# One fused SSM and gated-GLU kernel: PSUM read two banks at a time, paired products, and a new order

## The chip, the cores and the metric

One core of a Trainium2 chip runs the whole program. The time is device microseconds, the median of several runs. The engines are TensorE (PE), VectorE (DVE), ScalarE (ACT), GpSimd (POOL) and SyncE (SP), which issues most of the DMAs. Each has its own queue and works through it in order. [...]

## The reference

A layernorm of x (2048 tokens, 512 channels) feeds two branches that are added to x: a diagonal state-space layer, computed as a convolution over the whole length, and a gated linear unit.

```python
xn = layernorm(x)                                   # 2048 x 512
# branch A: K[d, l] = Re sum_n C[d,n] * exp(dt*A)[d,n]**l * (dt*B)[d,n],  128 modes, l = 0..2047
y  = irfft(rfft(pad(xn)) * rfft(pad(K)))[:L] + xn * Dskip
# branch B: 512 -> 1792 -> 512
h  = sigmoid(xn @ w_gate) * (xn @ w_up)
out = x + y + h @ w_down
```

Inputs and outputs are bfloat16; sums on PE are float32.

## The kernel before, in words

**Branch B** works on four groups of 512 tokens. For each group and each of 14 blocks of 128 hidden columns PE makes a gate product (L1031, four matmuls of 128x512) and an up product (L1046), each in one PSUM bank. ACT takes the sigmoid of the gate bank into `hT_sb` (L1040). DVE multiplies by the up product (L1061), straight from its bank or, for the blocks in the list `UEV`, from a copy `us_sb` that ACT has made of it (L1057). Then come the down products (L1090), 14 matmuls for each of four blocks of 128 tokens.

**Branch A** does the long convolution by transforms written as matmuls. A ladder of complex squares (ACT L656, DVE L665 and L667, twelve levels) gives powers of the decay; POOL's DMAs cast them into tables. From these DVE builds two factor tables G and H in four chunks of 128 channels (L722 to L728 products, L775 to L781 squares, seeds copied by `copy`, L291 and L293). PE multiplies them (L806), ACT brings the result to SBUF, PE selects and transposes it (L827). On the other side PE makes the first transform of the layernormed tokens (L684), ACT evacuates it, and SP writes it to DRAM (`z_scr`) and reads it back in another layout. For 8 unit pairs in two channel halves PE then makes a second step (L874) and the kernel's transform from streamed constants E (L890), ACT or DVE evacuates both, DVE multiplies them (L895, L899), sums some parts (L906, L907, L909) and PE makes the third step (L923, L935). How much is summed on DVE is the table `SUMS`: at level 0 PE gets 64 matmuls a pair, at level 1 32, at level 2 16. ACT's copies of that go to DRAM (`v_scr`) and come back, and PE makes the last transform (L999); DVE adds it to branch B (L1014, L1110), and the sum is stored.

**PSUM** has eight banks of 512 float32 columns. Each is a tile of its own, and every evacuation reads one bank: `halves` makes two copies of 128x512 out of two banks.

**The order** is written out by hand. `_Plan.add` lists 981 operations with the bank or buffer slots that each takes and gives back; the table `ORDER` says in which order they are handed to the engines, and `run` gives out slots first come, first served as it goes along that order. `ON_DVE` and `ON_ACT` name operations that change the engine, `WARM` the warm-up matmuls (L520) on a zero tile. So all of an engine's queue, and which bank a product gets, follows from these tables.

```python
def halves(dst, srcs, deps, prio, hold):
    cps = []
    for n, sl in enumerate(srcs):
        cps.append(pl.copy(nc, 0.48, lambda n=n: dst(n), lambda sl=sl: bank(sl), deps + cps, prio, acq=[] if n else [hold], rel=[sl]))
    return cps
```

## Time and profile before

| | |
|---|---|
| runs | 214.62, 214.68, 215.55 us; median 214.68 |
| profiled execution | span 212.7 us (first to last instruction); its own time is not on the page |
| busy | PE 204.5 us, DVE 196.0, ACT 176.8, POOL 40.5 |
| DMA | 42.35 MB, 199 GB/s in the mean |
| costliest | evacuations by ACT L293 81.5 us; gate products 53.8, up 53.1, down 50.4 |

"Busy" is time in which an engine had an instruction running; for PE the ends are modelled, so that a busy stretch can still hold gaps. DVE's and ACT's instructions are shown with a tail that overlaps the next one; the distance from one start to the next start is what an instruction takes from its queue. The releaser of a wait is what ended it last. The chain of waits is followed back from the last instruction, so it tells what could not have been earlier, and not all that was busy.

### The profile page before, as it was taken

Reading aid. Unit: us, or ns where it says so; the run is one execution under the profiler, and the core shown is the slowest. Engines: PE = TensorE matmul, PEld = TensorE weight load, DVE = VectorE, ACT = ScalarE, POOL = GpSimd, SP = SyncE. Lnnn points to the kernel's source line nnn. Section 1 sums busy time; section 2 is a strip of 40 time slices with the busy share of each in tenths; the row PEclk is TensorE's granted clock in tenths of the full one; section 3 lists DMA queues with packets and bytes.
Section 4 is the critical chain, followed back from the end, with each engine's and each line's share of the span. In section 5 each row is a group of like instructions: output and inputs, shape, how many; then the busy total and the mean of one; then the engine's idle time right before and its main releaser. Section 6 shows DMA issues by size and latency. Waiting matters only on the chain.

```text
span 212.7 us, 5732 instructions
## 1 busy us (share of the span) xinstructions
PE 204.5 (96%) x2226; PEld 103.6 (49%) x2251; DVE 196.0 (92%) x420; ACT 176.8 (83%) x364; POOL 40.5 (19%) x66
## 2 busy tenths in 40 slices
PE   7999999999999999999999999999999999999993
PEld 2574444444444354545456555644565446444442
DVE  3999999999999999999999999999999989984781
ACT  3999999999999999969999999898589999644000
POOL 4206033149877000002000002000040000000110
PEclk9999999999999999999999999999999999999999
DMA  6999937992995927987626446602899996778842
GB/s 205 385 411 349 292 85 166 195 205 33 195 201 195 208 98 223 145 250 265 151 70 216 125 152 166 160 6 60 256 306 222 329 303 188 206 216 230 248 158 91
DMA packets 44044, 42.35 MB, mean 199 GB/s; under 512 B 8809, under 2 KB 37746, under 8 KB 44018
## 3 DMA queue, kind: packets, MB, share of 16 engines
q1 hardware_dynamic: 39074, 36.95, 56.7%
q0 software_dynamic: 4512, 4.73, 14.3%
q8 instruction: 17, 0.28, 0.6%
q10 hardware_dynamic: 432, 0.33, 0.5%
q14 instruction: 9, 0.07, 0.1%
HBM read 25.21 MB, written 12.07 MB: 175 GB/s over the span
## 4 chain that ended last, share of the span: by engine, by line
PE 58%; ACT 33%; DMA 3%; issue 2%; DVE 1%; SPq 0%; POOL 0%; ACTq 0%; POOLq 0%
PE bank L1090 17%; PE bank L1046 11%; ACT big L293 10%; PE bank L1031 8%; PE bank L890 7%; ACT hT_sb L1040 7%; ACT big L656 5%; DMA xnT<-x_scr 3%; PE bank L806 3%; PE bank L520 3%; ACT glu_sb L536 2%; PE bank L923 2%; PE bank L999 2%; PE bank L935 2%; ACT glu_sb L535 2%
## 5 line engine op out<-in xcount | busy, mean ns | idle before, releaser
L293 ACT ACTIVATE big<-bank 128x512 bf16<-128x512 f32 (+2 forms) x147 | 81.5, 655 | 6.1 <-PE bank L806 2.5
L1031 PE MATMUL bank<-xnT,wg_sb 128*128 128x512 bf16 (+1 forms) x234 | 53.8, 361 | 1.2 <-ACT xnT L293 0.4
L1046 PE MATMUL bank<-xnT,wu_sb 128*128 128x512 bf16 x216 | 53.1, 379 | 0.8 <-ACT us_sb L1057 0.2
L1090 PE MATMUL bank<-wd_sb,hT_sb 128*128 128x512 bf16 (+1 forms) x231 | 50.4, 366 | 0.6 <-DVE hT_sb L1061 0.2
L1040 ACT ACTIVATE hT_sb<-bank 128x512 bf16<-128x512 f32 x56 | 34.7, 655 | 1.0 <-PE bank L1031 1.0
L1031 PEld LDWEIGHTS <-wg_sb 128*128 128x128 bf16 x244 | 22.8, 98 | 25.4 <-issue 4.5
L1090 PEld LDWEIGHTS <-hT_sb 128*128 128x128 bf16 x238 | 22.6, 98 | 25.5 <-issue 2.3
L1046 PEld LDWEIGHTS <-wu_sb 128*128 128x128 bf16 x224 | 21.4, 98 | 26.3 <-issue 2.1
L722 DVE TENSOR_TENSOR big<-big 128x1024 bf16<-128x1024 bf16 (+4 forms) x40 | 26.7, 667 | 0.2
L723 DVE TENSOR_TENSOR big<-big 128x1024 bf16<-128x1024 bf16 (+4 forms) x40 | 26.5, 663 | 0.0
L1057 ACT ACTIVATE us_sb<-bank 128x512 bf16<-128x512 f32 x31 | 21.8, 703 | 3.1 <-DVE rz L970 2.4
L895 DVE TENSOR_TENSOR big<-big 128x2048 bf16<-128x2048 bf16 x16 | 19.4, 1221 | 1.3 <-ACT big L293 0.6
L890 PE MATMUL bank<-big 128*128 128x256 bf16 x160 | 19.7, 273 | 0.6 <-ACT big L293 0.4
L890 PEld LDWEIGHTS <-big 128*128 128x128 bf16 x160 | 15.3, 98 | 5.7 <-DMA big<-c_E 1.1
L661 POOL DMA_DIRECT2D big<-big x24 | 13.0, 550 | 23.1 <-DVE big L667 14.4
L293 ACT ACTIVATE big<-big 128x256 bf16<-128x256 bf16 x34 | 16.8, 520 | 0.2 <-PE bank L806 0.2
L775 ACT ACTIVATE sq_sb<-big 128x256 bf16<-128x256 bf16 (+2 forms) x20 | 14.6, 744 | 2.7 <-DVE big L728 2.0
L727 DVE TENSOR_TENSOR big<-big 128x512 bf16<-128x512 bf16 (+4 forms) x40 | 16.5, 413 | 0.0
L728 DVE TENSOR_TENSOR big<-big 128x512 bf16<-128x512 bf16 (+4 forms) x40 | 16.5, 412 | 0.0
L1061 DVE TENSOR_TENSOR hT_sb<-hT_sb,bank 128x512 bf16<-128x512 bf16 x25 | 16.4, 677 | 0.0
L1061 DVE TENSOR_TENSOR hT_sb<-hT_sb,us_sb 128x512 bf16<-128x512 bf16 x31 | 12.9, 419 | 1.3 <-ACT us_sb L1057 1.3
L495 POOL TENSOR_TENSOR ln_ri<-ln_ve,half 128x4 f32<-128x4 f32 (+2 forms) x6 | 10.8, 1795 | 10.7 <-ACT ln_ve L537 8.4
(99 smaller groups left out, 222.2 us busy)
## 6 DMA issues: line engine op xcount, KB each, us to landing
big<-c_E SPq DMA_DIRECT2D x16, 320.0 KB, 5.0
z_scr<-big SPq DMA_DIRECT2D x16, 256.0 KB, 3.1
big<-z_scr SPq DMA_DIRECT2D x16, 256.0 KB, 3.8
v_scr<-big SPq DMA_DIRECT2D x16, 256.0 KB, 3.6
big<-big POOLq DMA_DIRECT2D x24, 128.0 KB, 3.5
big<-in_A_u_dram SPq DMA_DIRECT2D x4, 512.0 KB, 7.7
big<-v_scr SPq DMA_DIRECT2D x4, 512.0 KB, 4.0
wu_sb<-in_B_w_up_dram SPq DMA_DIRECT2D x2, 896.0 KB, 10.1
```

The lines of the kernel that those rows point to most:

```text
L293: nc.scalar.activation(out=get(out), in_=get(in_), func=ACT.Identity)
L722: V.tensor_tensor(out=wide(outp), in0=wide(lo), in1=mre, op=ALU.mult)
L723: V.tensor_tensor(out=wide(tb()), in0=wide(lo), in1=mim, op=ALU.mult)
L727: V.tensor_tensor(out=outp[:, :, 0], in0=outp[:, :, 0], in1=tb()[:, :, 1], op=opr)
L890: T.matmul(bank(sk[kt == NKT - 1])[:, DW * c:DW * c + DW], es()[:, c, kt, :], kT[p][:, kt, :], start=kt in (0, NKT - 1), stop=kt >= NKT - 2)
L895: V.tensor_tensor(out=pp()[:, :, 0:4, :], in0=xx()[:, :, 0, :].unsqueeze(2).to_broadcast([128, 2, 4, DW]), in1=kb().unsqueeze(1).to_broadc ...
L1031: T.matmul(bank(sl)[:, c0:c1], w_at(w, CUT_G, kt, k), xnT[:, grp, kt, c0:c1], start=(kt == 0), stop=(kt == KT - 1))
L1040: S.activation(out=hT_sb[:, hs.idx, k % 2, :], in_=bank(sl), func=ACT.Sigmoid)
L1046: T.matmul(bank(sl), w_at(wu_sb, CUT_U, kt, k), xnT[:, grp, kt, :], start=(kt == 0), stop=(kt == KT - 1))
L1057: S.activation(out=us_sb[:, us.idx, :], in_=bank(sl), func=ACT.Identity)
L1061: V.tensor_tensor(out=h(), in0=h(), in1=us_sb[:, us.idx, :] if on else bank(sl), op=ALU.mult)
L1090: T.matmul(bank(po)[:, 0:c[1] - c[0]], hT_sb[:, hts[k // 2].idx, k % 2, jj * 128:(jj + 1) * 128], wd_sb[:, k, c[0]:c[1]], start=first and ...
```

## The change

- The eight banks become one tile `banks`, and `joint(a, b)` is a view of 1024 columns where two slots are neighbours. Operations with `pairs=True` get neighbouring slots; single ones are taken by preference from slots without a free neighbour (`LONE`).
- `halves`, the two copies after L806 and the two after L827 become one instruction each that reads both banks, on ACT or DVE.
- Up and gate products are handled by pairs of blocks: `UPS` says for each of the 28 pairs whether ACT copies both, one or none of the up products, and whether DVE multiplies 512 or 1024 columns at once; `GATES` names three pairs whose sigmoid reads both banks. The matmuls are the same.
- The last transform is made for each channel half by itself (24 matmuls of 512 columns become 48 of 256), and DVE adds in place, so that the output buffer there falls away.
- Layernorm tiles 2 and 3 are normalized one by one; `ON_ACT` moves the statistics of six tiles to ACT, not seven, and tile 1 instead of 2 among the first four. Seeds are copied three groups at a time, `LAG0`, `EXP` and the list of `squares` are rearranged for that. The loads of E wait for the lower powers only (`w_low`). `SUMS` of the second half goes from (1, 2, 1, 1) to (1, 1, 2, 2).
- `ORDER` is another one, of 896 operations.

```diff
-SUMS = ((0, 0, 0, 1), (1, 2, 1, 1))
+SUMS = ((0, 0, 0, 1), (1, 1, 2, 2))
...
-UEV = (5, 11, 15, 16, 18, 21, 22, 24, 25, 27, 28, 29, 30, 31, 32, 33, 34, 35, 36, 37, 38, 39, 41, 42, 43, 44, 45, 47, 49, 53, 54,)
-ON_DVE = (95, 96, 97, 109, 118, 181, 194, 375, 485, 488, 494, 507, 551, 587, 598, 600,)
-ON_ACT = (2, 8, 9, 10, 11, 13, 15,)
+UPS = (2, 0, 0, 0, 0, 2, 0, 2, 5, 2, 6, 5, 0, 2, 4, 2, 4, 3, 2, 6, 3, 2, 0, 6, 3, 4, 4, 5)
+GATES = (0, 10, 15)
+ON_DVE = (99, 100, 101, 102, 112, 170, 180, 181, 182, 262, 434, 508, 797)
+ON_ACT = (1, 6, 8, 9, 11, 14)
 ORDER = [
-    1, 21, 23, 0, 24, 25, 29, 30, 2, 35, 26, 19, 27, 3, 5, 6, 31, 34, 43, 44, 32, 28, 36, 10, 14, 20, 22, 37, 40, 38, 33,
+    0, 2, 3, 6, 10, 14, 24, 25, 7, 4, 26, 36, 27, 21, 1, 5, 30, 31, 32, 42, 23, 33, 19, 28, 11, 43, 9, 48, 44, 34, 49,
...
+    def _pair(self, free, a, b):
+
+        best = min(((max(i, free.index(x + 1)), x) for i, x in enumerate(free) if x + 1 in free), default=None)
+        a.idx, b.idx = (best[1], best[1] + 1) if best else free[:2]
...
-            for s in op.acq:
-                s.idx = self.free[s.pool].pop(0)
+            for n, s in enumerate(op.acq):
+                free = self.free[s.pool]
+                if s.pool == "b" and op.pairs:
+                    if n % 2 == 0:
+                        self._pair(free, s, op.acq[n + 1])
+                elif s.pool == "b":
+                    at = min(range(len(free)), key=lambda i: i + LONE * (free[i] - 1 in free or free[i] + 1 in free))
+                    s.idx = free.pop(at)
...
-    banks = [psum.tile([128, 512], F32, name="bank%d" % i) for i in range(NBK)]
+    banks = psum.tile([128, 512 * NBK], F32, name="banks")
...
+    def joint(a, b):
+        return banks[:, 512 * a.idx:512 * a.idx + 1024] if b.idx == a.idx + 1 else None
...
-        cps = []
-        for n, sl in enumerate(srcs):
-            cps.append(pl.copy(nc, 0.48, lambda n=n: dst(n), lambda sl=sl: bank(sl), deps + cps, prio, acq=[] if n else [hold], rel=[sl]))
-        return cps
+        def parts(v, each):
+            return v if joint(*srcs) is not None else [each(n) for n in range(2)]
+        return [pl.copy(nc, 0.96, lambda: parts(dst(), lambda n: dst()[:, 512 * n:512 * n + 512]),
+                        lambda: parts(joint(*srcs), lambda n: bank(srcs[n])), deps, prio, acq=[hold], rel=srcs)]
...
     layernorm(1, 2, 1.05)
-    layernorm(2, 4, 1.1)
+    layernorm(2, 3, 1.1)
+    layernorm(3, 4, 1.15)
...
-            le = dma("SP", es, cten["E"].ap()[u], deps=w_use[0], prio=QP - 0.5, acq=[esl], pkt=2560, hv=0.9)(320 * KB)
+            le = dma("SP", es, cten["E"].ap()[u], deps=w_low[0], prio=QP - 0.5, acq=[esl], pkt=2560, hv=0.9)(320 * KB)
...
+        for p in range(NP):
+            sl = _Slot("b")
+            part = res[:, :, DW * p:DW * p + DW]
+
+            def fy(sl=sl, p=p):
+                for r in range(2):
+                    s2_mm(t, r, bank(sl)[:, DW * r:DW * r + DW], True, (DW * p, DW * p + DW))
+
+            def fe(sl=sl, part=part):
+                V.tensor_tensor(out=part, in0=bank(sl).rearrange("p (r d) -> p r d", r=2), in1=part, op=ALU.add)
...
+            cps = {0: (), 1: (), 2: (0, 1), 3: (0, 1), 4: (0,), 5: (1,), 6: (0, 1)}[mode]
...
+                    for x in [None] if len(do) == 2 and (cps or joint(*ub) is not None) else do:
+                        src = u2v() if x is None and cps else joint(*ub) if x is None else half2(u2v(), x) if x in cps else bank(ub[x])
+                        o_ = h2() if x is None else half2(h2(), x)
+                        V.tensor_tensor(out=o_, in0=o_, in1=src, op=ALU.mult)
```

What the tables do is seen in the queues. First ACT at the start, from the statistics of its first layernorm tile to the table load ahead of the sines (`xnT` are the copies of transposed tiles, L609/L638 and L615/L644 two steps of the decay's phase and size). Before:

```order
L535 ACTIVATE glu_sb,mv<-big 128x512
L536 ACTIVATE glu_sb,mv<-big,mv 128x512
L537 ACTIVATE ln_ve<-mv,eps 128x1
L602 ACTIVATE big<-big 128x512
L293 ACTIVATE xnT<-bank_66 128x4x128
L293 ACTIVATE xnT<-bank_67 128x4x128
L609 ACTIVATE big<-big,magic 128x512
L293 ACTIVATE xnT<-bank_70 128x4x128
L293 ACTIVATE xnT<-bank_63 128x4x128
L615 ACTIVATE big<-big 128x512
L618 ACT_TABLE_LOAD
```

Now:

```order
L557 ACTIVATE glu_sb,mv<-big 128x512
L558 ACTIVATE glu_sb,mv<-big,mv 128x512
L559 ACTIVATE ln_ve<-mv,eps 128x1
L631 ACTIVATE big<-big 128x512
L298 ACTIVATE xnT<-banks 128x4x128 x2
L638 ACTIVATE big<-big,magic 128x512
L644 ACTIVATE big<-big 128x512
L298 ACTIVATE xnT<-banks 128x4x128 x2
L647 ACT_TABLE_LOAD
```

The exponential stands ahead of the copies of tiles 2 and 3 now, and the first three rows are those of tile 1, not 2. On PE the eight transposes of these two tiles are split: ahead of each four stand eight gate halves of 256 columns, and the four warm-up matmuls between them are gone.

They stand further down on PE, among the last up products of group 0 (L1108, L1046 before), ahead of the last-but-one first transforms of that stretch (L711, L684 before). Before:

```order
L1046 MATMUL bank_68<-xnT,wu_sb 128x512
L684 LDWEIGHTS big
L684 MATMUL bank_69<-big 64x512
...
L684 MATMUL bank_67<-big 64x512
L1090 LDWEIGHTS hT_sb
L1090 MATMUL bank_65<-wd_sb,hT_sb 128x512
```

Now, as one piece:

```order
L1108 MATMUL banks<-xnT,wu_sb 128x512
L542 LDWEIGHTS glu_sb
L542 MATMUL banks<-glu_sb 128x512
...
L1108 LDWEIGHTS wu_sb
...
L542 MATMUL banks<-glu_sb 128x512
L711 LDWEIGHTS big
L711 MATMUL banks<-big 64x512
...
L1083 MATMUL banks<-xnT,wg_sb 128x512
L1161 LDWEIGHTS hT_sb
```

Two warm-up matmuls stand on each side of the last up product, and a gate product of group 1 (L1083) comes ahead of the first down products (L1161). Last, ACT in the second channel half, where the second step and the kernel's transform are evacuated. Before:

```order
L293 ACTIVATE big<-bank_68 128x512
L293 ACTIVATE big<-bank_63 128x512
L293 ACTIVATE big<-bank_66 128x512
L293 ACTIVATE big<-bank_65 128x512
L293 ACTIVATE big<-bank_67 128x512
L293 ACTIVATE big<-bank_64 128x512
L1040 ACTIVATE hT_sb<-bank_68 128x512
```

Now:

```order
L298 ACTIVATE big<-banks 128x1024
L1099 ACTIVATE hT_sb<-banks 128x512 x2
L298 ACTIVATE big<-banks 128x1024 x5
L1099 ACTIVATE hT_sb<-banks 128x512
L298 ACTIVATE big<-banks 128x1024 x3
```

Two rows of 512 have become one of 1024, and both banks come back after it.

## The prediction

> **What bounds the kernel now.** I read the page's busy table first, then its 40 slices.

> ```profile
> span 212.7 us, 5732 instructions
> PE 204.5 (96%) x2226; PEld 103.6 (49%) x2251; DVE 196.0 (92%) x420; ACT 176.8 (83%) x364; POOL 40.5 (19%) x66
> DVE  3999999999999999999999999999999989984781
> ACT  3999999999999999969999999898589999644000
> ```

> The span is 212.7 us and the three runs have a median of 214.68, so 1.98 us lies outside the span; the page prints no other time of its execution. A measurement of this kernel tells a change from none from about 0.5%, 1.07 us. PE is busy for 204.5 us. VectorE (DVE) and ScalarE (ACT) are nearly full as well up to slice 33 (176 us), and have room only after that. Next, four stretches of the span (the pairs are each engine's busy time and instructions, then comes the granted clock), and the longest waits of PE alone:

> ```profile
> 0.00:20.00 20.00, 18.22 (x101) 10.01 (x103) 15.80 (x38) 15.98 (x27) 6.29 (x20) 1.00 0.92 340
> 20.00:60.00 40.00, 39.20 (x194) 17.26 (x197) 39.83 (x95) 39.61 (x83) 19.27 (x25) 1.00 0.80 172
> 20.00:200.00 180.00, 176.95 (x2062) 88.25 (x2084) 173.66 (x372) 160.78 (x338) 32.62 (x44) 1.00 0.72 187
> 200.00:212.70 12.70, 9.36 (x66) 5.31 (x65) 6.58 (x12) 0.00 (x0) 1.59 (x2) 0.98 0.40 148
> ...
> PE bank L520 <- POOL glu_sb L506: 1.4, 1, 1.4
> PE bank L890 <- ACT big L293: 0.4, 1, 0.4
> PE bank L1031 <- ACT xnT L293: 0.4, 1, 0.4
> ```

> From 20 to 200 us PE is busy for 176.95 of 180 us at the full clock: 3.05 us are idle. So PE is the bound, and what ACT and DVE save is worth only what PE waits for them. The chain of waits runs along ACT as far as 66 us, but PE beside it was still busy. Its pieces also give PE's own pace:

> ```profile
> 15.80 2.06 ACT hT_sb L1040 x4
> 64.27 1.95 ACT big L293 x4
> 74.30 0.39 PE bank L1031
> 92.90 3.02 PE bank L1090 x14
> 180.10 0.79 PE bank L935 x32
> 174.58 0.64 PE bank L935 x16
> 196.10 1.42 PE bank L999 x12
> 205.74 0.56 PE bank L999 x6
> ```

> Fourteen down products take 3.02 us, 0.216 each. At the paces of the chain's pieces PE's list, from its first gate product at 8.84 us to its end at 209.5, adds up to about 195.3 of 200.6 us (my sum, with 0.1 us for each entry into a tiled group). So at most some 5.3 us could be won from PE by better order, 4.6 of it after the start; the 3.05 us of idle are the part that the view shows, the rest is hand-over inside pieces called busy.

> **The change, part by part.** *Wider evacuations.* ACT reads two neighbouring banks at once, 128x1024. No such row exists here; the nearest are these of ACT and DVE, in order of time:

> ```profile
> 106.01 0.61 ACT L293 ACTIVATE big<-bank 128x512 bf16<-128x512 f32 x1
> 106.96 1.39 ACT L293 ACTIVATE big<-bank 128x384 bf16<-128x384 f32 x3
> 108.18 0.66 ACT L1057 ACTIVATE us_sb<-bank 128x512 bf16<-128x512 f32 x1
> 17.87 0.94 ACT big L656
> 102.35 0.41 DVE L1061 TENSOR_TENSOR hT_sb<-hT_sb,us_sb 128x512 bf16<-128x512 bf16 x1
> 102.68 0.45 DVE L722 TENSOR_TENSOR big<-big 128x512 bf16<-128x512 bf16 x1
> 105.07 0.69 DVE L722 TENSOR_TENSOR big<-big 128x1024 bf16<-128x1024 bf16 x1
> 105.67 0.68 DVE L723 TENSOR_TENSOR big<-big 128x1024 bf16<-128x1024 bf16 x1
> ```

> From start to start 512 columns from PSUM take 0.47 us (0.49 over the chain's four), and 384 take 1.22/3 = 0.41; by these the slope is 0.5 to 0.8 ns a column, and 1024 would cost 0.75 to 0.90. From the other side stand 0.94 to 0.95 for 1024 columns in SBUF and 0.97 for two of 512. I take 0.90, nearest to the upper rows, against 0.96: some 0.06 us for each of 66 pairs, 4 us. The eight pairs of table evacuations, the seed copies in three groups and one layernorm tile handed to DVE add some 2 us; ACT's list goes from 355 instructions to 267 and, by these paces, from 173.5 to 168 us. On DVE one 1024-column product costs 0.60 against two of 0.33: 11 pairs, 0.8 us. Some copies of 512 go to ACT, one layernorm tile (1.0 us) and seed copies come; DVE's list falls from 194 to 192.5 us. All of that is beside PE, so its own worth is nothing; it acts through waits.

> [...]

> *PE's own work.* No product goes away. The last step of one unit pair is summed on DVE first (16 matmuls for 32: 0.64 for 0.79, -0.15 us). The last transform by channel halves turns 24 matmuls of 512 columns into 48 of 256: 12 in 1.42 less 0.1 for entry are 0.110 each, and 0.56 less 0.1 less two of 0.110 leaves 0.06 for each of the four of 256, so +0.2 (0 to +1).

> *Four warm-up matmuls move.* They stood at 7.5 us, where PE had nothing else:

> ```profile
> 4.68 0.63 ACT L535 ACTIVATE glu_sb<-big 128x512 bf16<-128x512 bf16 x1 [1.68 <-DMA big<-in_A_u_dram]
> 7.53 1.03 PE L520 MATMUL bank<-glu_sb 128*128 128x512 bf16 x4
> 8.39 0.61 PE L565 MATMUL bank<-ident,big 128*128 128x128 bf16 x8
> 8.84 1.04 PE L1031 MATMUL bank<-xnT,wg_sb 128*128 128x256 bf16 x8
> 10.23 8.97 PE L1031 MATMUL bank<-xnT,wg_sb 128*128 128x256 bf16 x55 [0.35 <-ACT xnT L293]
> 12.01 0.63 ACT big L618
> 14.51 1.28 ACT L1040 ACT_TABLE_LOAD   x1
> ```

> Now they stand among the last up products of group 0, at some 34 us: 4 x 0.216 = 0.86 us of nothing. It is free where PE would wait there. Behind them PE needs gate products of group 1, whose transposed input I put at 36 to 37.5 us, and then the products of group 0 by DVE; PE would be there at about 36. I take +0.5 (0 to 0.86).

> *The start.* Tile 1 in place of tile 2 has its statistics on ACT and so starts when its own load lands (some 3.5 us, not 4.68), and tiles 2 and 3 are normalized apart. PE's list now goes 8 transposes, 8 gate halves, 4 transposes, 8 halves, 4 transposes. The first gate product may come at 8.4 to 8.6 instead of 8.84. But ACT's copies of tiles 2 and 3 now wait for 16 gate halves on PE (0.109 each): from 8.5 us on, two times 0.87 for these and two times 0.3 for four transposes make 10.85; one copy more is 11.35; the table load (1.28), the four sines (12.01 to 14.51, 2.5) and the second load (1.28) end at 16.4. That is the first sigmoid, which stood at 15.80. With 40 halves and 12 whole gate products PE has filled all eight banks at about 16.3 (10.23 + 32 x 0.109 + 12 x 0.216), and its next product waits for that sigmoid, the one after the next for a third, behind a square of 0.94. From -0.3 (no wait) to +1.2 (a second wait of 0.6); I take +0.6.

> *Waits that go.* Rows of the list of waits, weight loads of PE with them:

> ```profile
> PEld L1031 <- DMA xnT<-x_scr: 0.5, 1, 0.5
> PEld L890 <- DMA big<-c_E: 1.1, 2, 0.9
> PEld L923 <- DVE big L899: 0.4, 2, 0.2
> PEld L935 <- DVE big L907: 0.4, 1, 0.4
> PEld L935 <- DVE big L906: 0.4, 1, 0.4
> 67.51 6.75 DMA xnT<-x_scr
> ```

> Gate products of group 2 waited at 74.3 us for the transposing DMA. In the new order that DMA is issued at about the same time (68 us), but its first reader stands some 4 us later: -0.6. The loads of E no longer wait for the whole tables, so -0.5 of the 1.1. The third step waited for DVE's products (three rows, 1.2 us). Adding up both lists, DVE's last sum stands 1.3 to 3.2 us ahead of PE's third step in seven of eight pairs before, and 5.5 to 10 now, for the kernel products stand earlier or DVE's other work later. Part of this is lent: for the first pair of the second half DVE's product now stands 4.4 us before the PE group that feeds it, where it was 0.6, so DVE will wait there instead. I take -0.9. With the 0.4 us of the kernel products' wait for ACT that makes -2.4, of which I hand back 0.4 for new places that cannot be seen: -2.0, between -4.6 (all of it) and +3.0 (the rival of the banks). Past 200 us nothing is won: PE's tail of 209.5 to 212.7 keeps its sum and its store.

> **Sum.** -0.15 + 0.2 + 0.5 + 0.6 - 2.0 = -0.85 us: span 211.85, and with 1.98 around it 213.8.

> **Rivals.** *Waits vanish.* PE runs dense: 0.6 us instead of 2.6 left over of the 4.6, so -4.0 in place of -2.0, and the warm-up matmuls fall into a wait: span 212.7 - 0.15 + 0.2 + 0.6 - 4.0 = 209.35, time 211.3; with -3.0 it is 212.3, which I take for this case. For it: DVE's lead of 5.5 us or more, and 6 us less on ACT. Against it: the order before had only 3.05 us idle.

> *Pairs starve PE of banks.* This is the side of slower. The third step, the kernel products, the first transforms and the table products now ask for two or four neighbouring banks at once, and a bank given to a pair comes back only when all 1024 columns are out: 0.90 - 0.48 = 0.42 us later than the first of two did. That is 78 pairs with 33 us of bank time. If one in six of PE's 150 or so groups of products stalls 0.2 us, that is +5.0 beside the -2.0: span 212.7 + 1.15 + 3.0 = 216.85, time 218.8; at half that rate 216.3, which I take. It decides from where PE's stalls behind evacuations sum to over 2 us. For it: eight banks, and PE asks for one about every 0.86 us. Against it: PE waited 0.4 us for such an evacuation so far. [...]

> *Two banks cost as much as two reads.* 128x1024 takes 0.95 or more, ACT saves 2 us in all, and the new order brings only its gains at fixed places (-0.6, -0.5) against the warm-up and the start (+1.1): span 212.75, time 214.7.

> **How the numbers follow.** The forecast gets 0.45, with a range of its own of 212.6 to 215.2, for the start and the warm-up can each be off by 0.6 and the waits by 1; four tenths of it lies below 213.6, over half within 1.07 us of 214.68. Vanished waits get 0.21, all faster. Starved banks get 0.20: slower in most of it. No gain by width gets 0.14, nearly all unchanged. Faster 0.18 + 0.21 + 0.01 = 0.40; slower 0.18 + 0.02 + 0.03 = 0.23; unchanged 0.37. The time is that of the forecast, 213.8; the range of 8 in 10 takes most of both sides in, 211.3 to 217.2.

> **What would show it.** Right: 128x1024 from PSUM at 0.88 to 0.92 us start to start; ACT near 170 us busy, DVE near 194; PE's idle from 20 to 200 us under 3 us with none for the transposing DMA; first sigmoid at 16.4 us or later; four warm-up matmuls near 35 us. Wrong: PE waiting for evacuations by more than 2 us in sum (starved banks), a first sigmoid before 15.8 (the start then gains), 128x1024 at 0.95, or third steps that wait for DVE as before.

## The result, and the profile after

The changed kernel takes 222.55 us (median of four runs, 221.54 to 224.18) against 214.97 for the kernel before beside it: 1.0368 of the time, with a 95% interval of 1.0319 to 1.0416 (the two medians alone give 1.035). It is 3.7% slower; 213.8 us had been predicted, and at most 217.2. The page of the profiled execution, and then stretches of it (busy time and instructions of PE, its weight loads, DVE, ACT and POOL; then granted clock, DMA share and GB/s):

```profile
span 219.8 us, 5636 instructions
...
PE 205.6 (94%) x2259; PEld 104.2 (47%) x2259; DVE 195.7 (89%) x409; ACT 172.5 (78%) x274; POOL 36.5 (17%) x67
...
q8 instruction: 17, 0.28, 0.6%
```

```profile
8.60:20.00 11.40, 9.92 (x69) 6.23 (x69) 10.63 (x22) 10.43 (x15) 2.23 (x3) 1.00 1.04 401
20.00:200.00 180.00, 173.24 (x2042) 85.98 (x2040) 168.84 (x356) 156.69 (x250) 28.94 (x45) 0.99 0.68 174
75.00:84.00 9.00, 6.43 (x150) 2.96 (x148) 9.00 (x20) 6.61 (x12) 0.00 (x0) 0.81 0.30 77
107.00:109.00 2.00, 1.32 (x83) 0.94 (x68) 2.00 (x8) 1.31 (x3) 1.75 (x6) 1.00 0.52 83
162.00:166.00 4.00, 1.31 (x82) 0.86 (x78) 1.54 (x4) 1.31 (x4) 1.73 (x2) 1.00 0.75 181
```

The total of busy time on PE has hardly moved (204.5 before). From 20 to 200 us PE now idles 6.76 us instead of 3.05, and three short stretches hold nearly all of it: 2.57 us at 75 to 84, 0.68 at 107 to 109, 2.69 at 162 to 166. Outside them 0.82 us are left. PE's own waits say what ended each:

```profile
PE banks L863 <- issue: 3.4, 2, 2.7
PE banks L711 <- ACT hT_sb L1099: 2.0, 2, 1.8
PE banks L1083 <- ACT xnT L298: 1.4, 2, 1.2
PE banks L1108 <- ACT hT_sb L1099: 1.2, 2, 0.8
PE banks L711 <- ACT big L1119: 0.8, 1, 0.8
```

"Issue" means that PE stood and the profile shows nothing that it waited for: 3.4 us of it in two of the four selection steps (L863). The waits of the first transform (L711) are the stop at 76 us. From 75 to 84 us the granted clock is 0.81 in the mean, and the eight matmuls behind the stop, of 512 columns, took 2.8 us where 0.216 each makes 1.7. Against the kernel before, the span's 7.1 us are then:

| | us |
|---|---|
| two stops in the selection steps | +3.4 |
| the stop at 76 to 79 us | +2.6 |
| the lower clock behind it | +1.1 |
| start: idle from the first gate product to 20 us 1.48 for 0.40, first gate product 0.24 earlier | +0.8 |
| all other waits of PE from 20 to 200 us, 0.82 for 3.05 | -2.2 |
| four warm-up matmuls at 35 us | +0.9 |
| the rest | +0.5 |

So what the change was predicted to win (2.0 us of waits) it did win, and at two places that the prediction did not have PE stood or ran slowly for 7 us. The table counts where PE's time went; what the end gains when a stop is taken away is another question, for the experiments.

### The profile page after: what moved, and what is told of

Read it like the earlier page. It is cut to its first block, busy times and chain, and to the rows that moved or that the text cites. A ratio compares the mean times of both kernels' runs of the same rounds, so it can differ in the third digit from the quotient of the medians.

```text
span 219.8 us, 5636 instructions
## 1 busy us (share of the span) xinstructions
PE 205.6 (94%) x2259; PEld 104.2 (47%) x2259; DVE 195.7 (89%) x409; ACT 172.5 (78%) x274; POOL 36.5 (17%) x67
## 4 chain that ended last, share of the span: by engine, by line
PE 65%; DVE 15%; ACT 6%; issue 5%; DMA 5%; POOL 2%; SPq 0%; ACTq 0%; DVEq 0%; POOLq 0%
PE banks L1161 17%; PE banks L1108 15%; PE banks L1083 13%; PE banks L931 8%; DVE hT_sb L1130 3%; DVE big L749 3%; DMA big<-big 3%; DMA big<-in_A_par_dram 2%; DVE big L750 2%; PE banks L834 2%; PE banks L915 2%; PE banks L964 2%; PE banks L1040 2%; DVE big L694 2%; PE banks L976 2%
## 5 line engine op out<-in xcount | busy, mean ns | idle before, releaser
L298 ACT ACTIVATE big<-banks 128x1024 bf16<-128x1024 f32 (+3 forms) x79 | 72.0, 952 | 11.2 <-PE banks L867 3.5
L1083 PE MATMUL banks<-xnT,wg_sb 128*128 128x512 bf16 (+1 forms) x244 | 55.1, 363 | 2.0 <-ACT xnT L298 1.4
L1108 PE MATMUL banks<-xnT,wu_sb 128*128 128x512 bf16 x224 | 55.8, 384 | 1.2 <-ACT hT_sb L1099 1.2
L1161 PE MATMUL banks<-wd_sb,hT_sb 128*128 128x512 bf16 (+1 forms) x238 | 50.1, 367 | 0.0
L1083 PEld LDWEIGHTS <-wg_sb 128*128 128x128 bf16 x244 | 23.1, 98 | 26.0 <-issue 5.3
L1161 PEld LDWEIGHTS <-hT_sb 128*128 128x128 bf16 x238 | 22.8, 98 | 25.4 <-issue 1.2
L1108 PEld LDWEIGHTS <-wu_sb 128*128 128x128 bf16 x224 | 21.0, 98 | 27.7 <-issue 5.5
L1099 ACT ACTIVATE hT_sb<-banks 128x512 bf16<-128x512 f32 (+1 forms) x53 | 31.8, 630 | 2.5 <-PE banks L1161 1.3
L1119 ACT ACTIVATE big<-banks 128x512 bf16<-128x512 f32 (+1 forms) x32 | 20.4, 651 | 2.3 <-DVE hT_sb L1130 1.7
L931 PE MATMUL banks<-big 128*128 128x256 bf16 x160 | 19.6, 273 | 0.0
L688 POOL DMA_DIRECT2D big<-big x24 | 13.6, 607 | 24.6 <-DVE big L694 16.9
L1130 DVE TENSOR_TENSOR hT_sb<-hT_sb,banks 128x512 bf16<-128x512 bf16 x21 | 14.0, 680 | 0.3 <-ACT big L298 0.3
L517 POOL TENSOR_TENSOR ln_ri<-ln_ve,half 128x1 f32<-128x1 f32 (+1 forms) x7 | 10.9, 1553 | 14.4 <-ACT ln_ve L559 10.6
L1130 DVE TENSOR_TENSOR hT_sb<-hT_sb,big 128x512 bf16<-128x512 bf16 (+1 forms) x24 | 12.9, 540 | 0.1
L683 ACT ACTIVATE big<-big 128x1024 f32<-128x1024 f32 x11 | 11.7, 1068 | 0.0
```

Of the source, the lines that this page charges most:

```text
L298: nc.scalar.activation(out=a, in_=b, func=ACT.Identity)
L931: T.matmul(bank(sk[kt == NKT - 1])[:, DW * c:DW * c + DW], es()[:, c, kt, :], kT[p][:, kt, :], start=kt in (0, NKT - 1), stop=kt >= NKT - 2)
L1083: T.matmul(bank(sl)[:, c0:c1], w_at(w, CUT_G, kt, k), xnT[:, grp, kt, c0:c1], start=(kt == 0), stop=(kt == KT - 1))
L1099: S.activation(out=o_, in_=i_, func=ACT.Sigmoid)
L1108: T.matmul(bank(sl), w_at(wu_sb, CUT_U, kt, k), xnT[:, grp, kt, :], start=(kt == 0), stop=(kt == KT - 1))
L1119: S.activation(out=o_, in_=i_, func=ACT.Identity)
```

## The experiments

"Measured" gives the ratio to the kernel before, run beside it, with its 95% interval, and the span of the one profiled execution. Executions of one kernel differ: their spans ran from 219.8 to 222.5 us for the changed kernel, and from 213.3 to 215.3 for the one with the start put back below. Spans of two single executions that lie 1 us apart therefore say little by themselves.

**Two suspects for each stop.** For the stops in the selection: either they belong to the place (transfers, banks or data there), or to PE's instructions. The queue named "instruction" brings 17 packets of 0.28/17 MB, some 16 KB each; PE's list has 4,518 matmuls and weight loads, and the two stops stand 1,788 of them apart, which is 7 blocks of 255.4. Seventeen blocks of that length, the first beginning at instruction 189, fit the list, and a packet appears near each block's beginning. The assumption to be tried is that a block is asked for only when the one before it is begun, so that PE stops wherever it works off a block faster than the next one arrives. At PE's paces (1.35 us for 128 table products, 0.56 for 16 of the second step, 0.79 for 64 of the selection, 0.216 for a wide one) the blocks that end in the two stops hold 2.6 us (78 table products, 4 up products, 16 of the second step, 29 of the selection) and 2.3 us of work (64 table products, 4 gate products, 59 of the selection). The shortest block of the kernel before, set off in the same way, holds 5.5 us.

```profile
159.32 1.42 PE L834 MATMUL banks<-big 128*32 128x82 bf16 x128
161.90 0.82 PE L863 MATMUL banks<-big,sw 128*32 128x96 bf16 x59
165.40 0.26 PE L863 MATMUL banks<-big,sw 128*32 128x96 bf16 x5 [2.69 <-issue]
...
107.17 0.52 PE L863 MATMUL banks<-big,sw 128*32 128x96 bf16 x29
108.37 0.56 PE L863 MATMUL banks<-big,sw 128*32 128x96 bf16 x35 [0.68 <-issue]
```

For the stop at 76 us: either pairs hold PSUM banks too long, or the tables come late. GpSimd's queue and VectorE's, first of the changed kernel, then of the kernel before:

```profile
48.08 1.05 POOL L688 DMA_DIRECT2D big<-big  x2 [1.78 <-DVE big L694]
49.14 6.08 POOL L517 TENSOR_TENSOR ln_ri<-ln_ve,half 128x4 f32<-128x4 f32 x1
55.98 3.70 POOL L688 DMA_DIRECT2D big<-big  x6
...
53.89 0.45 DVE L755 TENSOR_TENSOR big<-big 128x512 bf16<-128x512 bf16 x1
55.26 0.16 DVE L521 SCALAR_TENSOR_TENSOR ln_nb<-mv,ln_ri 128x4 f32<-128x4 f32 x1 [0.91 <-POOL ln_ri L517]
61.61 1.09 DVE L749 TENSOR_TENSOR big<-big 128x1792 bf16<-128x1792 bf16 x1 [3.72 <-DMA big<-big]
```

```profile
47.37 6.84 POOL L495 TENSOR_TENSOR ln_ri<-ln_ve,half 128x4 f32<-128x4 f32 x1
53.24 0.67 DVE L1061 TENSOR_TENSOR hT_sb<-hT_sb,bank 128x512 bf16<-128x512 bf16 x1
```

The power of the last layernorm group, on four columns, takes 6.08 us where the two others of that size take 1.0 and 1.1, and the casts of the power ladder queue up behind it: six are issued in one row at 55.98. VectorE runs out of work and idles 0.91 and 3.72 us for them. The kernel before has a power of 6.84 us too, but there VectorE had other operations: it was busy for 39.83 of the 40 us from 20 to 60.

**The blocks shifted in the kernel before.** Nothing but the warm-up is touched (the tiny matmuls are 56):

```diff
-                T.matmul(bank(wsl), glu_sb[:, 0, 0:128], glu_sb[:, 0, :], start=True, stop=True)
+                T.matmul(bank(wsl)[:, 0:432], glu_sb[:, 0, 0:128], glu_sb[:, 0, 0:432], start=True, stop=True)
+                for _ in range(4 if n > 6 and k < 5 else 3):
+                    T.matmul(bank(wsl)[0:32, 0:16], glu_sb[:, 0, 0:32], glu_sb[:, 0, 0:16], start=True, stop=True)
```

> The kernel before, with nothing changed but its warm-up matmuls at the start: each is 432 columns wide instead of 512 and is followed by three or four tiny ones (56 in all, 32x16), which puts 112 more instructions ahead of everything TensorE does later. The order, the banks and all other work stay. Theory 'instruction blocks': TensorE's instructions come in blocks of some 255 by a queue of their own, the next block is asked for when one is begun, and it takes 3.4 us (quiet) to 5.4 us (busy transfers), so TensorE stops wherever it works off a block in less. With 112 more instructions two blocks fall on the second and third table products (L806 in the kernel before), 125 and 126 of their 128 matmuls and two others, worked off in 1.75 us each: TensorE then stops twice, right at the end of the second and just after the third table products, 1.6 to 3.6 us each, and the profiled span grows from 212.7 to 215.9 to 219 us. Theory 'the place': the two stops in the selection steps of the changed kernel came from the transfers, banks or data around them and not from the count of instructions; then this kernel stops nowhere new and its span stays within 0.6 us of 212.7.

Measured: 1.0336 (1.0301 to 1.0371), span 221.0. (Lines stand two lower in this kernel and in the next one of its kind.)

```profile
134.33 1.41 PE L808 MATMUL bank<-big 128*32 128x82 bf16 x128
135.68 0.39 PE L1048 MATMUL bank<-xnT,wu_sb 128*128 128x512 bf16 x1
138.32 2.32 PE L1048 MATMUL bank<-xnT,wu_sb 128*128 128x512 bf16 x10 [2.26 <-issue]
...
169.22 0.75 PE L876 MATMUL bank<-big,m 64*32 64x512 bf16 x16 [1.22 <-issue]
```

One of the two stops came, 2.26 us long and at the place named, in the up products behind the third table products. The other did not: PE began the second table products at 102.71 us and the gate products behind them at 104.22 without one. That block begins just ahead of the table products, behind 18 matmuls of 512 columns; why PE did not stop there is not shown. A third stop, of 1.22 us, came where none had been worked out, ahead of a second step (L876, last row). By the count a block begins there too. The one before it began at 163.5 us and holds some 4.5 us of work: more than the 3.4 us of the expectation's quiet case, less than its 5.4 for busy transfers, and less than the 5.7 us that passed until the second step ran at 169.22. And the span says little, for the tiny matmuls between the wide ones slowed the warm-up: the first gate product came at 14.3 us instead of 8.84. A cleaner trial was needed, with one bunch in place of the four late warm-up matmuls:

```diff
-WARM = (2, 2, 2, 2)
+WARM = (-56, 2, 0, 2)
...
+            for _ in range(-n):
+                T.matmul(bank(wsl)[0:32, 0:8], glu_sb[:, 0, 0:32], glu_sb[:, 0, 0:8], start=True, stop=True)
```

> The kernel before again with its instruction blocks shifted, this time without slowing the start: the four warm-up matmuls that run at 7.5 us are replaced by one bunch of 56 tiny ones (32x8), which moves everything later by 104 instructions and leaves the thirteen early warm-ups as they are. Theory 'instruction blocks': a block now begins at the third matmul of the second table products and ends one gate matmul behind them (1.54 us of work), and one begins at the seventh matmul of the third and ends six up matmuls behind them (2.57 us); a fetch that is asked for inside a table product took 3.2 to 5.5 us in the three stops seen so far, so TensorE stops 1.6 to 4 us in the gate matmuls (L1032) behind the second table products and 0.6 to 3 us in the up matmuls (L1047) behind the third, the span grows from 212.7 by 2.2 to 7 us. Theory 'the place': no stop over 0.5 us on TensorE, and the span within 0.8 us of 212.7.

Measured: 1.0147 (1.0102 to 1.0192), span 215.4. (L1032 and L1047 of the expectation are L1033 and L1048 here.)

```profile
98.04 1.46 PE L808 MATMUL bank<-big 128*32 128x82 bf16 x128
99.43 0.39 PE L1033 MATMUL bank<-xnT,wg_sb 128*128 128x512 bf16 x1
102.00 2.32 PE L1033 MATMUL bank<-xnT,wg_sb 128*128 128x512 bf16 x10 [2.18 <-issue]
...
131.53 1.41 PE L808 MATMUL bank<-big 128*32 128x82 bf16 x128
132.87 1.25 PE L1048 MATMUL bank<-xnT,wu_sb 128*128 128x512 bf16 x4
134.86 1.67 PE L1048 MATMUL bank<-xnT,wu_sb 128*128 128x512 bf16 x7 [0.73 <-issue]
```

Both stops stand where they were put, after one gate matmul (2.18 us) and among the up matmuls (0.73 us), in places where the kernel before never stopped, and the span grew by 2.7 us for 2.9 us of stops. At these places nothing but the number of instructions ahead was different; the start differed a little, with the first gate product at 9.52 us instead of 8.84. So the count of instructions alone makes such stops. That the two of the changed kernel are of this kind follows from their places by the same count, and from the next experiment.

**The selection steps moved away from the table products.** Two pieces of `ORDER`; 250 and 332 are the second and fourth selection, 714, 735, 864, 868 and 815 gate and up products, 426 a second step, 785 to 797 evacuations:

```diff
-338, 250, 293, 714, 346, 347, 294, 262, 735, 251, 348, 369, 744,
+338, 293, 714, 346, 347, 294, 262, 735, 250, 251, 369, 744, 348,
...
-331, 785, 447, 854, 332, 795, 797, 426, 787, 333, 864, 418, 434, 429, 427, ... 422, 868, 451, ... 479, 815,
+331, 785, 787, 795, 797, 447, 854, 426, 864, 427, 868, 332, 815, 333, 434, 418, 429, ... 422, 451, ... 479,
```

> The changed kernel, with fillers put between its second and fourth table products and the selection steps behind them (8 gate matmuls ahead of the second selection; 16 second-step, 4 gate and 4 up matmuls ahead of the fourth, with the copies that free their banks). No work is added or removed, the instruction count ahead of the steps stays. Theory 'instruction blocks': the two blocks worked off in 2.6 and 2.3 us now last 4.2 us each; the stop of 0.68 us in the second selection goes, that of 2.69 us in the fourth goes or shrinks to about 1.2 us, and the profiled span falls from 219.8 by 2.0 to 3.4, to 216.4 to 217.8 us. Theory 'the place': the stops stay with their steps, and the span stays within 0.7 us of 219.8.

Measured: 1.0343 (1.0297 to 1.0390), span 220.2. (Here and in all later kernels lines stand two above those of the changed kernel.) The stops went as the blocks say; the time did not. What remains of the fourth's stop, and then the same place in the next kernel, which leaves the selections alone but runs 5 us earlier:

```profile
164.54 0.56 PE L861 MATMUL banks<-big,sw 128*32 128x96 bf16 x35
165.47 0.52 PE L861 MATMUL banks<-big,sw 128*32 128x96 bf16 x29 [0.37 <-issue]
```

```profile
156.54 0.82 PE L861 MATMUL banks<-big,sw 128*32 128x96 bf16 x59
160.18 0.34 PE L861 MATMUL banks<-big,sw 128*32 128x96 bf16 x5 [2.83 <-issue]
```

With fillers the block ends after the 35th selection matmul, by count, and there the 0.37 us stand. Without, it stops after the 59th again, whatever the time of day. But PE's waits for ACT's copies grew in exchange: L913 waits 1.0 us, L929 0.9 and L1081 1.3 (0.6 in the changed kernel) for evacuations and sigmoids that come late behind the later selections. So the stops were turned into other waits; the expected 2.0 to 3.4 us did not come, although in this run the clock did not fall behind the stop at 76 us either.

**The ladder's cast ahead of the power.** In `ORDER`, 84 and 90 are casts, 121 the power, 122 the operation on it, 608 the accumulating DMA:

```diff
-152, 121, 122, 648, 628, 682, 88, 649, 608, 114, 629, 153, 84, 90, 17, 664, 617, 89, 176, 650
+152, 84, 121, 608, 648, 628, 682, 88, 649, 114, 629, 153, 90, 17, 664, 617, 89, 176, 122, 650
```

Two theories stand against each other: the power of 6.08 us holds up the casts, VectorE then idles 0.91 and 3.72 us for them, and the late tables make PE stop at 76 us; or the banks do.

> The changed kernel, with one cast transfer of the power ladder put ahead of the last layernorm power (L517) in GpSimd's queue, the accumulation and the other casts behind it, and the small VectorE operation that needs the power three VectorE operations later. [...] Then VectorE idles under 1.5 us between 54 and 62, the first table products start 2.5 to 4.5 us earlier than 82.55, TensorE has no stop over 0.8 us between 70 and 84, and the span falls from 219.8 by 2.5 to 3.8, to 216.0 to 217.3 us. Theory 'banks': TensorE stops at 76 because sigmoid and up copies of pairs hold the banks, whatever the ladder does; then the stop stays and the span stays within 0.7 us of 219.8.

Measured: 1.0159 (1.0108 to 1.0210), span 216.2: 3.6 us less, as expected; the ratio falls by 0.021, 4.5 us.

```profile
50.94 1.05 POOL L686 DMA_DIRECT2D big<-big  x2 [1.87 <-DVE big L692]
52.01 3.16 POOL L515 TENSOR_TENSOR ln_ri<-ln_ve,half 128x4 f32<-128x4 f32 x1
...
54.20 0.67 DVE L1128 TENSOR_TENSOR hT_sb<-hT_sb,banks 128x512 bf16<-128x512 bf16 x1
56.75 1.07 DVE L747 TENSOR_TENSOR big<-big 128x1792 bf16<-128x1792 bf16 x1
```

VectorE's product of 1792 columns starts at 56.75 instead of 61.61 with no idle time ahead, PE idles 0.34 us from 70 to 84 us, and the clock stays at 1.00 there. No bank was touched, so the stop at 76 us was the ladder's. Behind the stop of 2.83 us at the fourth selection, shown above, the clock now fell instead: it was 0.91 in the mean from 152 to 162 us, where the changed kernel had kept 1.00 around and behind its own stop (162 to 170 us).

**Both edits.**

> The changed kernel with both edits: fillers between table products and selections, and the ladder's cast ahead of the layernorm power. If the two causes are separate and are what made the changed kernel slow, the gains add: the span falls from 219.8 by 4.5 to 7.2, to 212.6 to 215.3 us, within 2.6 us of the kernel before. If one of the delays only hid another (the ladder's lateness was absorbed later, or the next wait takes its place), the span stays over 216 us.

Measured: 1.0152 (1.0127 to 1.0177), span 215.9. The gains do not add. On top of the cast, fillers take away two stops of 3.1 us together and the slow clock behind the second, and the span falls by 0.3 us. New waits of PE for ACT, 1.0 us in L913 and 1.1 in L929, take back part of it; where the rest went is open.

**Fillers at one place.** The same without the first piece of the diff on the selections:

> The changed kernel with the ladder's cast ahead of the power, and with fillers ahead of the fourth selection alone: the second selection is left where the change has it, and its stop of 0.31 us stays. Both edits with fillers at both places gave 215.9 us, hardly less than 216.2 without fillers, although the stop of 2.83 us was gone. Theory 'the second filler costs': the second selection, 1.5 us later, delays its copy and the kernel transforms behind it (TensorE waits 0.74 us more in 100 to 120 us than without it); then the span falls to 214.4 to 215.3. Theory 'the fourth gives its gain back': the delayed fourth selection makes the copies pile up at 164 to 169 us, and the span stays at 215.6 to 216.4.

Measured: 1.0135 (1.0080 to 1.0191), span 215.0. That is 0.9 us of span less, as the theory of the second filler says, but the ratios lie within each other's intervals. The same holds against the cast alone (1.0159, 216.2 us): no run shows for certain that taking away the selection's stops makes the changed kernel faster.

**The warm-up matmuls left out** (`WARM = (0, 2, 0, 2)`), on the kernel with both edits:

> The changed kernel with both edits (fillers, and the ladder's cast ahead of the power), and without the four warm-up matmuls that the change runs at some 34 us instead of at the start: they are left out altogether. If TensorE's list of work sets the end there, the end comes earlier by their 0.86 us: the span falls from 215.9 to 214.8 to 215.3. If TensorE has slack that these matmuls only fill (it waits for banks or for the ladder soon after them anyway), the span stays at 215.6 to 216.2.

Measured: 1.0190 (1.0148 to 1.0232), span 217.1. No gain; but every block began 8 instructions earlier in the work (L861 stops 0.6 us again) and the start was worse (PE busy for 15.53 us of the first 20 instead of 16.00), so it was tried again below.

**The width undone**, on the same kernel:

```diff
-        return banks[:, 512 * a.idx:512 * a.idx + 1024] if b.idx == a.idx + 1 else None
+        return None
```

> The changed kernel with both edits, and with every joined evacuation by 1024 columns (58 on ScalarE, two on VectorE) and the table and selection evacuations made as two reads of one bank each, in the same place and order: only the width is undone. The rows give 0.48 us from start to start for 512 columns and 0.92 to 1.05 for 1024, so two reads cost as much as one. Theory 'width is worth nothing': the span stays within 0.8 us of 215.9. Theory 'width saves ScalarE': 60 evacuations save 0.06 us or more each, 3.6 us of ScalarE's time in a stretch where TensorE waits for it, and the span grows by over 1 us. Theory 'two banks held too long': a bank is free after 0.48 us instead of after both have been read, and the span falls by over 0.8 us.

Measured: 1.0187 (1.0141 to 1.0233), span 217.3, against 1.0152 (1.0127 to 1.0177): not told apart, and tried again below on a quieter base.

**The start put back.** 37 and 43 are the variances of tiles 2 and 3, 39 and 45 their normalizations, 40 and 46 their transposes, 41 and 47 the copies, 49 and 50 VectorE's products with the timestep, 53 ACT's square:

```diff
-43, 9, 48, 44, 34, 49, 29, 8, 37, 35, 50, 529, 531, 45, 46, 541, 51, 553, 53, 38, 39, 40, 15, 543, 47, 96, 41, 52,
+43, 37, 9, 48, 44, 38, 34, 49, 29, 8, 35, 45, 39, 50, 529, 46, 40, 531, 541, 51, 47, 553, 41, 15, 543, 53, 52, 96,
```

> The changed kernel with the ladder's cast ahead of the power, fillers ahead of the fourth selection, and its start put back into the order that the kernel before has: the variances of the third and fourth tile before VectorE's first product with the timestep (which waits for the parameters), both normalizations before its second, and the two tiles' transposes and copies side by side ahead of the second group of gate matmuls. Theory 'the start': the third and fourth tile arrive 0.9 to 2.1 us later in the changed kernel than before, TensorE waits 0.8 to 1.2 us for them and 1.2 us for the sigmoids behind them; then TensorE is 1 to 1.7 us busier in the first 20 us than with the same edits without this (15.67), the first sigmoid runs at 15.7 to 16.2 us instead of 16.9, and the span falls from 215.0 to 213.3 to 214.2. Theory 'slack': what TensorE gains at the start it loses again at its next wait for the ladder or for banks, and the span stays at 214.6 to 215.4.

Measured: 1.0063 (1.0039 to 1.0087), span 214.4. First rows of the changed kernel in order of time; then VectorE's same product, the first sigmoid and the first 20 us of the kernel without this edit (fillers at one place, start as in the change); then the first 20 us and the first sigmoid of this one:

```profile
6.94 0.63 ACT L631 ACTIVATE big<-big 128x512 bf16<-128x512 bf16 x1 [1.20 <-DMA big<-in_A_par_dram]
7.61 0.69 DVE L633 TENSOR_TENSOR big<-big 128x512 f32<-128x512 bf16 x1 [0.49 <-ACT big L631]
8.21 0.17 DVE L566 BATCH_NORM_AGGREGATE mv<-stats 128x2 f32<-128x6 f32 x1
16.91 1.09 ACT L1099 ACTIVATE hT_sb<-banks 128x512 bf16<-128x512 f32 x2
```

```profile
6.93 0.69 DVE L631 TENSOR_TENSOR big<-big 128x512 f32<-128x512 bf16 x1
16.21 1.09 ACT L1097 ACTIVATE hT_sb<-banks 128x512 bf16<-128x512 f32 x2
0.00:20.00 20.00, 15.67 (x92) 8.55 (x94) 15.51 (x35) 15.90 (x26) 6.36 (x20) 1.00 0.92 341
```

```profile
0.00:20.00 20.00, 16.79 (x93) 9.15 (x95) 15.36 (x35) 16.16 (x26) 5.90 (x20) 1.00 0.92 340
15.94 1.09 ACT L1097 ACTIVATE hT_sb<-banks 128x512 bf16<-128x512 f32 x2
```

In the changed kernel the variance of tile 2 (8.21) stands on VectorE behind a product that waits for ACT's exponential, which waits for the parameters. In the kernel without this edit the parameters landed earlier; the same product waited for nothing, and the first sigmoid came at 16.21 us in the same order of the start. So of the 0.97 us between 16.91 and 15.94 about 0.7 come from when a transfer landed, and 0.27 are left against the edit's own base. Counted from the first gate product, which came at 8.60, 7.93 and 8.37 us, the sigmoid came 8.3 us later in both kernels with the changed order and 7.6 us later with the order put back. This 0.7 us is the order's, and it does not hang on the wait for the parameters. Which of the moved operations saves it was not tried: the edit moves variances, normalizations, transposes and copies together. The ratio falls by 0.0072 (1.5 us), the profiled span by 0.6, to 214.4, between the two theories; the two intervals overlap by a hair. Some 0.6 to 1.5 us is the best estimate of the start's price.

**A smaller second filler** (250 behind 714):

> The same with four gate matmuls (not eight) ahead of the second selection too: its instruction block lasts 3.4 us instead of 2.6, about the fetch time of 3.2 to 3.9 us seen inside table products. If what is left of the stop there (0.3 to 0.8 us) is all that can be had, the span is 0 to 0.6 us under that of the kernel without it.

Measured: 1.0100 (1.0071 to 1.0128), span 215.2. Not better, rather worse: filling ahead of the second selection costs more than its stop.

**Width and warm-up again, on this base.** The first is the diff of the width above; in the second the four matmuls keep their instructions but have 8 columns.

> The best of the kernels so far (ladder's cast ahead of the power, fillers ahead of the fourth selection, start put back; 214.4 us of span, 1.0063 of the time before), with the width undone alone: every joined evacuation of 1024, table or selection columns is made as two reads of one bank each, in the same place and order. The first trial of this, on another base, gave 1.0187 against 1.0152, within the scatter. Theory 'width is worth nothing': the ratio stays within 0.002 of 1.0063. Theory 'width saves ScalarE': 0.06 us each on 60 evacuations, where TensorE waits for ScalarE (its waits for copies and sigmoids sum to some 4 us); the ratio grows to 1.009 or more. Theory 'two banks held too long': it falls to 1.003 or less.

> The same best kernel with the four warm-up matmuls that the change runs at some 34 us cut from 512 columns to 8, so that their instructions still count and every instruction block begins where it did. Left out altogether on another base the time did not fall (1.019 against 1.0152), but there the blocks had moved by 8 instructions and the start's transfers had come late. Theory 'on the path': 4 x 0.2 us go, the span falls from 214.4 to 213.4 to 213.9 and the ratio to 1.001 to 1.004. Theory 'only filler': TensorE waits the longer at its next wait for banks or the ladder; the ratio stays within 0.002 of 1.0063.

Measured: 1.0068 (1.0043 to 1.0093) with a span of 214.5 for two reads of one bank, and 1.0078 (1.0047 to 1.0108) with 213.9 for the short warm-up. Both lie on the 1.0063 of their base. The width saves ScalarE time, 175.5 us busy without it and 172.6 with it, and none of that reaches the end, as far as intervals of some 0.5 us to either side can tell. The moved warm-up matmuls are filler.

The best of these kernels is 0.63% slower than the kernel before; none beats it. Of that rest, 0.9 us on PE's list are the warm-up matmuls that leaving out did not win back, and PE idles 4.87 us from 20 to 200 us instead of 3.05; 1.4 us of it are waits for ACT's copies around the fourth selection (155 to 168 us), 0.9 one wait for a copy at 64.5 us. Which of these waits sets it was not tried.

## Why the prediction was wrong

It forecast 213.8 us with 0.45 and gave slower 0.23. Its terms, one by one:

**Width: right in price and in worth, too high in sum.** 128x1024 from PSUM was put at 0.90 us from start to start. The rows:

```profile
31.97 1.95 ACT L298 ACTIVATE big<-banks 128x1024 bf16<-128x1024 f32 x2
33.78 0.62 ACT L1099 ACTIVATE hT_sb<-banks 128x512 bf16<-128x512 f32 x1
```

Two take 1.81 us, 0.905 each, against 0.48 for a bank alone. ACT fell by 4.3 us to 172.5 us busy, where some 7 us, to near 170, had been forecast; DVE is at 195.7 (194). That all of it is worth nothing by itself, as the prediction said, the run with the width undone bears out within its interval: 1.0068 for 1.0063.

**PE's own work: right.** Twenty matmuls of the last transform by halves take 1.21 us, 0.0605 each, where 0.06 was worked out.

**Four warm-up matmuls (+0.5, between 0 and 0.86): the low end.** They stand at 35.49 and 36.79 us as forecast; making them short gained nothing that can be measured.

**The start (+0.6, between -0.3 and +1.2): about right.** By the table it cost 0.8 us; put back, it is worth 0.6 us by the spans and 1.5 by the ratios. The first sigmoid came at 16.91 us, and at 16.21 in another kernel with the same order of the start, on either side of the forecast's 16.4. The mechanism came as counted: ACT's copies of tiles 2 and 3 waited for PE (0.15 and 0.61 us ahead of them in the changed kernel), and PE then waited 0.77 and 0.46 us for the first sigmoids. That tile 2's variance now stands behind a product that can wait for the parameters was not counted; no run shows that it mattered.

**Waits that go (-2.0): right in sum, partly by luck.** Outside the three stops PE's idle time from 20 to 200 us fell from 3.05 to 0.82 us, by 2.2. The waits for the transposing DMA and for the loads of E are gone. But -0.9 of the sum was put on the third step, and its weight loads still wait for VectorE as they did (1.2 us before):

```profile
PEld L976 <- DVE big L948: 0.6, 2, 0.4
PEld L976 <- DVE big L950: 0.4, 1, 0.4
```

So the size came out right with one of its parts wrong; what made it up is spread over hand-overs that no single row shows.

**The step that failed: what the new order costs PE at its new places, set at +0.4; PE stood or ran slowly there for 7 us.** The sum took PE's time as paces of matmuls plus waits on semaphores, "no product goes away", and handed back 0.4 us for new places that cannot be seen. Two things stood there instead.

The first is that it had no term for PE's instructions. The new order puts table products, a second step and a selection next to each other, blocks of some 128 matmuls, nearly all small, in 2.3 to 2.6 us of work, where no block of the kernel before held less than 5.5. PE stood 3.4 us there. In the kernel before, 2.9 us of such stops made the span 2.7 us longer; in the changed kernel the fillers that took the stops away won nothing by themselves (220.2 us for 219.8) and 0.3 to 1.2 us of span on top of the cast, within the scatter. So what they cost the changed kernel in the end is not shown. Both orders were to be had, and a count of small matmuls per stretch would have shown the place; that such a stretch stops PE no row of the kernel before could show, for it never stopped there.

The second is a failure to read, and the larger part: 3.6 us of span, 4.5 by the ratio, went when one cast was put ahead of the power and two small operations with it were moved. The prediction followed SP's loads, ACT, DVE and PE, but not GpSimd's queue. There the kernel before already showed a power of 6.84 us with the casts behind it, and the new order of VectorE showed that after the casts' products nothing else was left for it to do. Row and order together pointed at the place.

**The rivals.** "Pairs starve PE of banks" (0.20) named the right side and its own sign came: PE's waits behind ACT sum to more than 2 us. But the largest of them went when the ladder was freed and no bank was touched, and reading each bank by itself did not make the kernel faster, 1.0068 against 1.0063, though PE's idle time from 20 to 200 us fell from 4.87 to 3.87 us with it. (Banks were still given out two neighbours at a time there; that part of the rival was not undone.) "Waits vanish" (0.21) put the waits that go at 4.0 us, where 2.2 went, and was wrong on the time. "Two banks cost as much as two reads" (0.14) was wrong on the price and would have been right on its worth.

## What to carry to other kernels

A new order is judged on every queue, the idle ones too: look for a long operation on a lightly loaded engine and ask what stands behind it and what the waiting engine has left to do. On a PE-bound kernel count the instructions as well as the time: where many small matmuls stand together, spread wide ones among them (here stops came at blocks of some 255 matmuls and weight loads with 1.5 to 4.5 us of work, and none in the kernel before, whose shortest block holds 5.5), and check that what is moved late is not awaited elsewhere. A stop that is removed by moving work is only won if nobody waits for the work that was moved.

## What the runs showed of the hardware

```profile
160.00:161.00 1.00, 0.80 (x79) 0.75 (x66) 1.00 (x3) 0.83 (x2) 0.00 (x0) 1.00 1.09 317
162.00:163.00 1.00, 0.71 (x59) 0.56 (x55) 1.00 (x4) 1.00 (x3) 0.00 (x0) 1.00 1.23 335
164.00:165.00 1.00, 0.00 (x0) 0.00 (x0) 0.00 (x0) 0.00 (x0) 1.00 (x2) 1.00 0.10 19
```

The DMA share was 1.09 to 1.23 while that packet was awaited at 160 to 163 us; it was 1.04 and 0.93 from 104 to 106 us too, where the other packet came after 0.9 us. What made the one late was not tried. From packet to first instruction 2.7 and 2.4 us passed in these two stops (105.7 to 108.37 and 163.0 to 165.40 us), the second with the DMA engines at 0.10 (164 to 165 us), and 2.4 to 2.8 us in the two of the shifted kernel without the slowed start.

**GpSimd's last power took 3.2 to 6.8 us.** That is the last group's power in the four kernels looked at: 6.84 us in the kernel before, 6.08 in the changed one, 3.16 with the cast moved, 3.17 with fillers at one place. In three of them it ended 0.97 us after VectorE had begun an operation with an operand in PSUM (at 53.24, 54.20 and 53.57 us), in the changed kernel 0.9 us after VectorE had fallen idle, which then itself waited 0.91 us for the power; until then VectorE had run operations on SBUF alone, nearly all with two operands there. Other powers were short beside such operations: the one of the kernel before at 17.45 us took 1.07 us, the one of the changed kernel at 41.62 us took 1.14. What held the last one is not shown.

**A clock that fell behind some stops.** In the changed kernel the granted clock was 0.50 from 78.4 to 81.8 us, beginning inside the second of two waits of 1.79 and 0.79 us with two matmuls between them, and in the kernel with the cast moved it was 0.91 in the mean from 152 to 162 us, around a stop of 2.83 us. It stayed at 1.00 from 75 to 84 us in the kernel with fillers alone, where PE idled 2.17 us, and from 162 to 170 us in the changed kernel, whose own stop of 2.69 us lies there. Why the one and not the other is open.
